# The last 96 rows of a weight matrix: one load of ScalarE, or six loads of GpSimd with unequal shares

## The chip, the cores and the metric

The kernel runs on one core of a Trainium2 chip. The metric is the device time of one launch in microseconds (us). The engines are called as in the profile: PE is TensorE's matmuls, PEld its weight loads, DVE is VectorE, ACT is ScalarE, POOL is GpSimd, SP is SyncE. Sixteen DMA engines move data between the chip's memory and the core's on-chip memory. The text calls them "DMA engines" throughout, to keep them apart from the compute engines that issue the loads.

## The reference

A decode step for two tokens (B = 2, D = 512) adds three terms: the input, an attention over a cache, and a bilinear feed-forward block.

```
xn = layernorm(x)
q  = xn @ wq                                  # 32 heads of 128
k, v = the last 2048 positions of the caches  # per token and head
A  = softmax(q k^T / sqrt(128)) v @ wo        # wo: 4096 x 512
g, u = xn @ w_gate, xn @ w_up                 # 512 x 1376
out = x + A + (g * u) @ w_down                # w_down: 1376 x 512
```

Everything is float32. w_down has 1376 = 10 * 128 + 96 rows: ten blocks of 128 rows, and a rest of 96. The change is about how those 96 rows get onto the chip.

## The kernel before

Nearly all inputs are laid out by the host into one array `stream`, in the order in which the kernel wants them. `loads()` lists the pieces: each entry is a load number, a tile (`step0` to `step2`, or `extra`) and its fields (two or three heads of the caches, slices of wq, wo, w_down). `issue()` puts these loads on SP's queue. A load is [128, up to 13824] float32, one long row for each of 128 partitions, spread over all 16 DMA engines. A load into a `step` tile has to wait on SP until that tile's last use has ended, so three loads at most are open at a time.

The compute engines follow the stream. For each head DVE multiplies the keys by q (`products`) and sums (`sums`), every fourth head gives the softmax weights of a group (`weights`, with ACT's exponentials), and PE multiplies the weights by the values (`weigh`) and adds the output projections into one accumulator `acc` in PSUM (`wo`, `down`). The stream ends with load 24, which is cut into five pieces so that little work is left behind the last one: the value rows of the last head, four blocks of wo, and blocks 1 to 9 of w_down. After the last piece there are a few small matmuls, a copy and the store of the result.

Three small things are not in `stream`. `x_nat`, the two rows of x, goes to the tile `xr`. `wd_rest`, the last 96 rows of w_down, goes to the tile `wr` (96 partitions, 2 KB in each). Both are loaded from ACT's queue, ahead of ACT's first computation. `wr` has one reader: the matmul in `turn()`, `add_rows(hT[:FR, ...], wr, 0)`, which adds those rows' share to `acc` in the third step of the loop, once the feed-forward block's hidden values `hT` are there.

`Program` records every operation and finds its dependences from the tiles' regions; `emit()` writes them out per engine, in the order recorded, with a semaphore for every load. A reader of a tile that several loads fill waits for each of those loads. All instructions are issued by two lines of `emit()`, so the profile gives them one line number, L198 (L199 in the changed kernel, which is one line longer above it).

Of the kernel before, what the change touches and what calls it, by code (L numbers as in the profile page):

```python
# [10 lines left out]
P = 128  # L11
B, D, H, DH, SK, F = 2, 512, 32, 128, 8192, 1376
# [7 lines left out]
NFC = F // P  # L20
# [7 lines left out]
M = 4 * N  # L28
CK, CO = J * DH, D
CX = B * NC + 4 * N + 4 * HG + 2 * NFB + 2 + B  # L30
BUFS = 3
WIDTH = 13824
WIDTH_X = 4096
# [2 lines left out]
def loads():  # L36
# [6 lines left out]
    def wq(g, *cs):  # L43
        return units("wq", *[(g, c) for c in cs])
# [8 lines left out]
    for n in range(6, 20):  # L53
# [29 lines left out]
    out = [  # L83
        (0, "x", [("c", 0, CX)] + wq(0, 0, 1, 2, 3)),
        (1, 0, big[1] + small[1]),
# [150 lines left out]
def build(nc, stream, x_nat, wd_rest, out):  # L236
    pr = Program(nc)
    pe, dve, act, pool = pr.pe, pr.dve, pr.act, pr.pool

    buf = [pr.sb(f"step{i}", [P, WIDTH]) for i in range(BUFS)]  # L240
    buf_x = pr.sb("extra", [P, WIDTH_X])
    xr = pr.sb("xr", [P, D])
    wr = pr.sb("wr", [FR, D])
# [7 lines left out]
    xnb = pr.sb("xnb", [P, NC, P])  # L251
    cst = pr.sb("cst", [P, CX])
    p_all = pr.sb("p", [P, 2, HG, JG, M])
# [22 lines left out]
    for n, t, fields in loads():  # L276
# [8 lines left out]
        src = stream[pos : pos + P * (c1 - c0)].rearrange("(p i) -> p i", p=P)  # L285
# [3 lines left out]
    def issue(upto):  # L289
        while queue and queue[0][0] <= upto:  # L290
            _, dst, src = queue.pop(0)
            pr.load("SP", dst, src)

    issue(3)
    pr.load("ACT", wr, wd_rest)
    dve.memset(mean_w, 1.0 / D)
    dve.memset(eps_t, EPS)
    dve.memset(ones, 1.0)
# [2 lines left out]
    for t in (xr, zero, mt, both, p_all):  # L301
        pool.memset(t, 0.0)
    pr.load("ACT", xr[:B, :], x_nat)

    c0 = got["c", 0]
    dve.tensor_copy(cst, c0)
# [264 lines left out]
    a, b, c, d = GROUPS[g]  # L571
# [31 lines left out]
def laid_out(x):  # L603

    import numpy as np

    a = x["A_x"].reshape(B, D)
    xs = np.zeros((P, CX), a.dtype)
    xs[:, : B * NC] = a.reshape(B, P, NC).transpose(1, 0, 2).reshape(P, B * NC)
    o = B * NC  # L610
    for r in range(4):
        for n in range(N):
            xs[4 * n + r :: 32, o + r * N + n] = 1.0
    o += 4 * N
    for n in range(HG):
        for q in range(4):
            xs[32 * q + n, o + 4 * n + q] = 1.0
    o += 4 * HG
    for n in range(NFB):
        for b in range(B):  # L620
            xs[32 * n + b, o + n * B + b] = 1.0
    o += 2 * NFB
    for j in range(4):
        for b in range(B):
            xs[32 * j + b, o + b] = 1.0
    xs[:, o + 2 :] = a[:, 0]
    cache = {
        kind: x[name][:, :, SK - W :, :].reshape(B, H, HB, J * DH).transpose(1, 0, 2, 3)
        for kind, name in (("k", "A_k_cache"), ("v", "A_v_cache"))
    }  # L630
    wq = x["A_wq"].reshape(P, NC, H * DH)
    wo = x["A_wo"].reshape(H, P, D)
    gu = {
        kind: x[name].reshape(P, NC * F)
        for kind, name in (("wg", "B_w_gate"), ("wu", "B_w_up"))
    }
    wd = x["B_w_down"]

    def field(kind, i):
        if kind == "c":  # L640
            return xs
        if kind in ("k", "v"):
            return cache[kind][i].reshape(P, CK)
        if kind == "wq":
            g, c = i
            return wq[:, c, g * HG * DH : (g + 1) * HG * DH]
        if kind == "wo":
            return wo[i]
        if kind == "wd":
            return wd[i * P : (i + 1) * P]  # L650
        return gu[kind]

    parts = [
        np.concatenate([field(kind, i) for kind, i, _ in fields], axis=1).ravel()
        for _, _, fields in loads()
    ]
    return {"stream": np.concatenate(parts), "x": a, "wd_rest": wd[NFC * P :]}


_INS = ["A_x", "A_k_cache", "A_v_cache", "A_wq", "A_wo", "B_w_gate", "B_w_up", "B_w_down"]  # L660
# [24 lines left out]
```

## Time and profile before

| what | value |
|---|---|
| median of 3 runs | 377.32 us (377.32 to 377.57) |
| the profiled execution | 377.64 us |
| its span, first to last instruction | 376.3 us |
| outside the span (377.64 - 376.3) | 1.3 us |
| busy: DVE, PE, ACT, POOL | 80%, 50%, 4%, 1% of the span |
| moved by the DMA engines | 159.66 MB, mean 424 GB/s |

The profile is one execution's page, with views that answer questions about parts of it. The views used below are the page's list of DMA queues, which gives packets, megabytes and the share of 16 DMA engines' time for each queue (also for a part of the span alone); the timeline, which lists instructions in order; the windows, which give each engine's busy time, the DMA engines' busy share and the rate for stretches of the span; and the chain of work that ended last. In the timeline a bracket at the end of a row tells how long the engine had been idle and what ended that. Queue q1 is SP's, q10 is ACT's; q8 and q14 bring instructions, not data.

### The profile page before, as it was taken

What the parts mean: (1) busy time and instruction counts of PE and PEld (TensorE: products, weight loads), DVE (VectorE), ACT (ScalarE), POOL (GpSimd) and SP (SyncE); (2) the same over time, 40 slices, a digit from 0 to 9 for tenths busy, and PEclk for the clock granted to TensorE, in tenths of its full rate; (3) what the DMA queues carried; (4) which work ended last, traced back from release to release, by engine and by line L of the source; (5) the groups of instructions that cost most, each with busy time, mean ns of one, the idle gap of its engine ahead of it and who ended that gap; (6) DMA issues with size and microseconds to landing.
All of it is one profiled execution on the core that took longest, in us unless ns stands there. A gap on an engine that the chain in (4) does not pass through costs nothing.

```text
span 376.3 us, 1954 instructions
## 1 busy us (share of the span) xinstructions
PE 189.3 (50%) x844; PEld 56.8 (15%) x844; DVE 302.8 (80%) x165; ACT 14.5 (4%) x28; POOL 2.6 (1%) x9
## 2 busy tenths in 40 slices
PE   0651747703762355617446383462657335243976
PEld 0210122100220011102121020110111012000312
DVE  3059979999999988899599499969969997999401
ACT  1000100000000000000000000000000001000100
POOL 2000000000000000000000000000000000000000
PEclk9956966876665658768555856858566685565999
DMA  8999899998999989999999999999999999999995
GB/s 324 470 394 488 376 470 411 431 470 377 464 435 417 464 382 460 453 400 464 394 448 453 406 458 400 447 454 406 453 420 419 445 447 434 441 402 411 432 416 235
DMA packets 4443, 159.66 MB, mean 424 GB/s; under 512 B 498, under 2 KB 626, under 8 KB 980
## 3 DMA queue, kind: packets, MB, share of 16 engines
q1 hardware_dynamic: 4320, 159.35, 98.5%
q10 hardware_dynamic: 116, 0.20, 0.1%
q8 instruction: 6, 0.10, 0.1%
q14 instruction: 1, 0.01, 0.0%
HBM read 159.49 MB, written 0.07 MB: 424 GB/s over the span
## 4 chain that ended last, share of the span: by engine, by line
DMA 49%; DVE 42%; PE 6%; issue 2%; another core or an unknown queue 1%; SPq 0%; DVEq 0%
DMA step<-in_stream_dram 49%; DVE step L198 22%; DVE s L198 19%; PE q L198 3%; PE o_ps L198 2%; PE acc L198 2%; PE tr L198 0%; DVE both L198 0%; DVE nm L198 0%; DVE h_sb L198 0%; DVE rec L198 0%; SPq L198 0%; DVE mt L198 0%; DVE o_out L198 0%
## 5 line engine op out<-in xcount | busy, mean ns | idle before, releaser
L198 DVE TENSOR_TENSOR step<-step,q 128x4096 f32<-128x4096 f32 x32 | 141.1, 4408 | 37.3 <-DMA step<-in_stream_dram 37.3
L198 DVE TENSOR_REDUCE s<-step 128x32 f32<-128x4096 f32 x32 | 141.4, 4418 | 0.8
L198 PE MATMUL o_ps<-step,p 128*32 128x512 f32 x496 | 94.8, 869 | 69.8 <-DMA step<-in_stream_dram 68.2
L198 PE MATMUL q<-step,xnb 128*128 128x512 f32 x56 | 41.4, 877 | 26.9 <-DVE step L198 19.7
L198 PE MATMUL acc<-step,oT 128*2 128x512 f32 x64 | 23.6, 926 | 42.2 <-DVE oT L198 28.5
L198 PEld LDWEIGHTS o_ps<-step,p 128*32 128x32 f32 x496 | 20.4, 147 | 126.8 <-DMA step<-in_stream_dram 74.9
L198 PEld LDWEIGHTS q<-step,xnb 128*128 128x128 f32 x56 | 13.4, 267 | 54.5 <-DVE step L198 24.9
L198 ACT ACTIVATE p<-s,zero 64x128 f32<-64x128 f32 x16 | 6.4, 399 | 268.1 <-DVE s L198 268.0
L198 DVE TENSOR_TENSOR oT<-gu,rec 128x8 f32<-128x8 f32 x8 | 1.3, 158 | 14.8 <-PE gu L198 14.8
L198 PE MATMUL tr<-both,ones 128*128 128x24 f32 (+1 forms) x18 | 4.8, 348 | 15.7 <-DVE both L198 15.7
L198 PE MATMUL gu<-step,xn 128*2 128x512 f32 (+1 forms) x48 | 8.5, 647 | 7.5 <-DMA step<-in_stream_dram 7.5
L198 PE MATMUL gu<-cst,o_sb 128*128 128x8 f32 x64 | 10.1, 285 | 3.1 <-ACT o_sb L198 3.1
L198 PEld LDWEIGHTS gu<-cst,o_sb 128*128 128x128 f32 x64 | 9.4, 225 | 10.6 <-ACT o_sb L198 8.9
L198 PEld LDWEIGHTS acc<-step,oT 128*2 128x2 f32 x64 | 1.5, 82 | 53.0 <-DVE oT L198 29.1
L198 PEld LDWEIGHTS tr<-both,ones 128*128 128x128 f32 x18 | 3.8, 262 | 26.6 <-DVE both L198 26.6
L198 PE MATMUL q<-extra,xnb 128*128 128x512 f32 x8 | 6.2, 947 | 1.9 <-DVE xnb L198 1.9
L198 DVE TENSOR_REDUCE nm<-tr 64x4 f32<-64x8 f32 x16 | 2.6, 163 | 5.4 <-PE tr L198 5.3
L198 ACT COPY o_sb<-o_ps 128x512 f32<-128x512 f32 x8 | 4.7, 585 | 46.0 <-PE o_ps L198 46.0
L198 PE MATMUL gu<-cst,h_sb 128*128 128x6 f32 x8 | 1.9, 362 | 5.6 <-DVE h_sb L198 5.6
L198 PE MATMUL tr<-st,mean_w 128*128 128x4 f32 x2 | 0.6, 365 | 7.5 <-DVE st L198 7.5
L198 PEld LDWEIGHTS gu<-step,xn 128*2 128x2 f32 x48 | 2.0, 93 | 14.7 <-DMA step<-in_stream_dram 9.1
L198 DVE TENSOR_REDUCE both<-p 128x8 f32<-128x256 f32 x8 | 3.3, 413 | 0.6 <-ACT p L198 0.6
(52 smaller groups left out, 39.8 us busy)
## 6 DMA issues: line engine op xcount, KB each, us to landing
step<-in_stream_dram SPq DMA_DIRECT2D x17, 6912.0 KB, 31.2
step<-in_stream_dram SPq DMA_DIRECT2D x2, 6400.0 KB, 29.5
step<-in_stream_dram SPq DMA_DIRECT2D x1, 6656.0 KB, 35.9
step<-in_stream_dram SPq DMA_DIRECT2D x1, 5504.0 KB, 34.4
step<-in_stream_dram SPq DMA_DIRECT2D x1, 4608.0 KB, 23.8
extra<-in_stream_dram SPq DMA_DIRECT2D x1, 2048.0 KB, 28.3
step<-in_stream_dram SPq DMA_DIRECT2D x1, 2048.0 KB, 24.8
step<-in_stream_dram SPq DMA_DIRECT2D x2, 1024.0 KB, 19.6
```

The costliest lines, as they stand in the source:

```text
L198: ins = getattr(e, method)(*args, **kw)
```

## The change

The one load of `wr` from ACT's queue is taken out. In its place POOL issues six loads, behind its five memsets. They fill 30, 8, 2, 22, 4 and 30 partitions of `wr`. The source of each is written as `(j i) d -> i j d`, which cuts its rows over 3, 2, 2, 2, 4 and 3 DMA engines, 16 in all, and the host reorders the rows of `wd_rest` to match. If each load goes on from the DMA engine at which the one before it ended, every DMA engine carries one share: three get 10 rows each, then two 4, two 1, two 11, four 1, three 10. Before, the 96 rows were cut evenly, 6 for each.

```diff
+REST = ((3, 30), (2, 8), (2, 2), (2, 22), (4, 4), (3, 30))
...
     issue(3)
-    pr.load("ACT", wr, wd_rest)
     dve.memset(mean_w, 1.0 / D)
...
     for t in (xr, zero, mt, both, p_all):
         pool.memset(t, 0.0)
     pr.load("ACT", xr[:B, :], x_nat)
+    lo = 0
+    for k, m in REST:
+        src = wd_rest[lo : lo + m, :].rearrange("(j i) d -> i j d", i=k)
+        pr.load("POOL", wr[lo : lo + m, :], src)
+        lo += m
...
-    return {"stream": np.concatenate(parts), "x": a, "wd_rest": wd[NFC * P :]}
+    rest, lo = [], NFC * P
+    for k, m in REST:
+        rest.append(wd[lo : lo + m].reshape(k, m // k, D).transpose(1, 0, 2).reshape(m, D))
+        lo += m
+    return {"stream": np.concatenate(parts), "x": a, "wd_rest": np.concatenate(rest)}
```

POOL's whole work in the kernel's body, before:

```order
L198 MEMSET xr 128x512
L198 MEMSET zero 128x1
L198 MEMSET mt 128x32
L198 MEMSET both 128x24
L198 MEMSET p 128x2048
```

and the end of it in the changed kernel:

```order
L199 MEMSET both 128x24
L199 MEMSET p 128x2048
L199 DMA wr<-in_wd_rest_dram 30x1x512
L199 DMA wr<-in_wd_rest_dram 8x1x512
L199 DMA wr<-in_wd_rest_dram 2x512
L199 DMA wr<-in_wd_rest_dram 22x1x512
L199 DMA wr<-in_wd_rest_dram 4x512
L199 DMA wr<-in_wd_rest_dram 30x1x512
```

The six loads stand behind everything else that POOL does; nothing is queued behind them.

PE around the one reader of `wr`, with what each row waits for (`s_d` with a number is the semaphore of one load), before:

```order
L198 MATMUL gu<-cst,h_sb 128x6 [waits s_DVE]
L198 MATMUL gu<-cst,h_sb 128x6 x3
L198 MATMUL q<-step,xnb 128x512 [waits s_d3]
L198 MATMUL acc<-wr,hT 2x512 [waits s_d4,s_DVE]
L198 MATMUL q<-step,xnb 128x512 x2
```

and in the changed kernel:

```order
L199 MATMUL gu<-cst,h_sb 128x6 [waits s_DVE]
L199 MATMUL gu<-cst,h_sb 128x6 x3
L199 MATMUL q<-step,xnb 128x512 [waits s_d3]
L199 MATMUL acc<-wr,hT 2x512 [waits s_d19,s_d18,s_d20,s_d17,s_d21,s_d16,s_DVE]
L199 MATMUL q<-step,xnb 128x512 x2
```

PE's order is the same; the matmul that reads `wr` waits for six loads where it waited for one. On ACT the load of `wr` is gone and the load of `xr` is the first instruction; DVE's and SP's orders are unchanged.

## The prediction

> **What bounds the kernel now.** I read the page's list of DMA queues first, then the windows over the whole span. The first shows how the 16 DMA engines' time is used (packets, MB, share of their time), the second whether they are ever idle (the last two columns are the DMA engines' busy share and GB/s; a transfer is counted where it starts).
>
> ```profile
> q1 hardware_dynamic: 4320, 159.35, 98.5%
> q10 hardware_dynamic: 116, 0.20, 0.1%
> ...
> 52.00:371.00 319.00, 164.36 (x721) 47.25 (x724) 271.07 (x139) 11.07 (x24) 0.00 (x0) 0.68 1.00 430
> ```
>
> SP's stream holds the DMA engines 98.5% of the time, and from 52 to 371 us their share is 1.00: no gap. So the time is the stream's bytes at the DMA engines' rate, a start and a tail. Compute matters only if it keeps SP from issuing. It doesn't, by the lead of the loads (KB each, us from issue to landing):
>
> ```profile
> step<-in_stream_dram SPq DMA_DIRECT2D x17, 6912.0 KB, 31.2
> ```
>
> 6912 KB are 7.08 MB, 16.5 us at 430 GB/s; landing after 31.2 us means that a load lies queued for some 14.7 us behind the one in flight. Compute can be late by about that before the DMA engines see it.
>
> The end is in the timeline, the result's last four instructions:
>
> ```profile
> 372.69 0.84 PE L198 MATMUL q<-step,hT 128*2 128x128 f32 x24
> 373.72 0.33 PEld L198 LDWEIGHTS q<-step,hT 128*2 128x2 f32 x16 [0.48 <-DMA step<-in_stream_dram]
> 373.72 0.62 PE L198 MATMUL q<-step,hT 128*2 128x128 f32 x16 [0.19 <-DMA step<-in_stream_dram]
> 374.41 0.29 DVE L198 COPY o_out<-q 128x128 f32<-128x128 f32 x1 [1.99 <-PE q L198]
> 374.73 0.35 SPq L198 DMA_DIRECT2D out_dram<-o_out  x1
> ```
>
> The last matmuls wait for the last piece of the stream, which lands just before 373.72; what follows is fixed. A load has landed when the slowest of its DMA engines is done, so the question is whether all 16 are done together. The windows at the end say no:
>
> ```profile
> 371.00:371.60 0.60, 0.60 (x8) 0.00 (x0) 0.00 (x0) 0.00 (x0) 0.00 (x0) 1.00 0.93 376
> 371.70:372.25 0.55, 0.00 (x0) 0.00 (x0) 0.52 (x1) 0.00 (x0) 0.00 (x0) 1.00 0.45 183
> 372.25:372.75 0.50, 0.27 (x12) 0.27 (x16) 0.17 (x1) 0.00 (x0) 0.00 (x0) 1.00 0.42 172
> 372.75:373.68 0.93, 0.78 (x31) 0.47 (x20) 0.00 (x0) 0.00 (x0) 0.00 (x0) 1.00 0.09 35
> ```
>
> From about 371.7 the share is 0.45 to 0.42 of 16, about seven DMA engines; nine have nothing left. The seven go on until the share falls to 0.09, so they end about 1 us after the nine. Which work made seven late? The list of queues for 6.3 to 371 us:
>
> ```profile
> q1 hardware_dynamic: 3889, 156.86, 99.7%
> q8 instruction: 6, 0.10, 0.1%
> q14 instruction: 1, 0.01, 0.0%
> ```
>
> Seven packets that are not the stream's: six instruction fetches of 16 KB and one of 8 KB. Seven fetches and seven late DMA engines: the simplest reading is one fetch each, six long delays and one shorter. The stream itself is even (128 rows on 16), and so were the 96 rows.
>
> **The change, part by part.** I add to the profiled execution, 377.64 us with a span of 376.3; it is 0.3 above the median of 377.32, so differences are carried over to the median.
>
> *a. The rows on the late DMA engines.* What one 2 KB row costs a DMA engine has two rows: the stream's (98.5% of 376.3 x 16 is 5930 us for 159.35 MB, 37 us per MB), and ACT's queue in the first 7 us, where the 96 rows and the two of x went:
>
> ```profile
> q10 hardware_dynamic: 116, 0.20, 8.1%
> ```
>
> 8.1% of 7.0 x 16 is 9.1 us for 0.20 MB, 45 us per MB. So a row costs 0.076 to 0.093 us. Six DMA engines get 1 row in place of 6, two get 4, eight get 10 or 11. If the six are the ones with the long fetches, and one of the two with 4 rows has the short fetch, the last to end saves 5 x 0.076 to 5 x 0.093, 0.38 to 0.46: I take **-0.42**. What is late next: the nine others get up to 5 rows more, 0.46, and had about 1 us of margin, so they don't take over. The pieces before the last one (values, wo, w_down) come off the same DMA engines and land earlier by as much, so the 0.19 us that PE had in hand at 373.72 is kept.
>
> *b. The first load without company.* SP's first load, 1057 KB of x, constants and wq, shared its DMA engines with the 96 rows:
>
> ```profile
> extra<-in_stream_dram SPq DMA_DIRECT2D x1, 1057.0 KB, 5.9
> ...
> 2.70:3.80 1.10, 0.00 (x0) 0.00 (x0) 0.12 (x1) 0.37 (x1) 0.44 (x1) 1.00 0.94 389
> 3.80:5.30 1.50, 0.00 (x0) 0.00 (x0) 0.00 (x0) 0.00 (x0) 0.00 (x0) 1.00 1.04 368
> ```
>
> It ran at 368 to 389 GB/s, not 430. If the small rows were the reason, its 1.08 MB take 2.5 us in place of 2.9: up to -0.42, for all DMA engines, since the rows then come between long rows. If its own shorter rows are the reason, nothing. The trace doesn't tell; I lean to the second and take **-0.1**.
>
> *c. Completions.* Six loads end where one did. If every DMA engine reports each of them, that is 5 more tiny packets on each. The nearest row is the very end, 372.5 to 376.3 us, where nearly all packets are small:
>
> ```profile
> q1 hardware_dynamic: 169, 0.14, 10.9%
> ```
>
> 10.9% of 3.8 x 16 is 6.6 us, 0.039 us a packet, of mostly 512 bytes and more. Five cost 0 to 0.2; I take **+0.1**.
>
> [...]
>
> *d. Issue and waits.* The load that goes (us to landing, then the issue on ACT), POOL's last memset, and the reader of `wr` on PE:
>
> ```profile
> wr<-in_wd_rest_dram ACTq DMA_DIRECT2D x1, 192.0 KB, 5.5
> ...
> 0.73 0.41 ACTq L198 DMA_DIRECT2D wr<-in_wd_rest_dram  x1
> ...
> 1.34 1.80 POOL L198 MEMSET p<- 128x2048 f32 x1
> ...
> 56.91 1.86 PE L198 MATMUL acc<-wr,hT 96*2 96x512 f32 x2 [2.47 <-DVE hT L198]
> ```
>
> POOL is free from 3.14 us and the rows are wanted at 56.91, when `hT` comes: 53 us. The load took 5.5 us to land from ACT's queue; six in a row from POOL, even at that time each, are there by 36 us. Were a row to be served only between two rows of the stream (55 KB at 37 us per MB, 2.06 us), 11 rows take 23 us more than that, about 59: then PE would wait some 2 us, with q's matmuls and the next softmax behind it, still inside the 14.7 us of lead. [...] ACT loses one issue of 0.41 us ahead of a wait; the first load's arrival a little earlier meets DVE, which then waits for the second load anyway:
>
> ```profile
> 6.64 0.20 DVE L198 COPY cst<-extra 128x66 f32<-128x66 f32 x1 [3.83 <-DMA extra<-in_stream_dram]
> ...
> 23.05 4.42 DVE L198 TENSOR_TENSOR step<-step,q 128x4096 f32<-128x4096 f32 x1 [13.11 <-DMA step<-in_stream_dram]
> ```
>
> All zero. **Sum:** -0.42 - 0.1 + 0.1 = -0.42, 377.64 to 377.22; from the median, **376.9 us**. About 0.2%, 0.75 us, is what a measurement of this kernel can tell from no change, so this counts as the same.
>
> **The rivals.**
>
> *Slower: each visit costs.* A queue that a DMA engine serves rarely may cost it more than its bytes. The fetches are the only such visits here; from 140 to 160 us there is one:
>
> ```profile
> q1 hardware_dynamic: 172, 8.63, 100.0%
> q8 instruction: 1, 0.02, 0.3%
> ```
>
> 0.3% of 20 x 16 is 0.96 us (0.8 to 1.1 by rounding), for 16 KB that the stream's rate moves in 0.61: 0.2 to 0.5 more. If each of the six loads, with its share or its completion, costs each DMA engine that, the stream ends 1.2 to 3.0 later, less the 0.42 saved: 378.1 to 379.9. It decides from 0.2 us a visit ((0.75 + 0.42) / 6). For it: POOL's queue is unused in the trace, and how its loads are served is unknown. Against: ACT's rows, also from a second queue, cost 0.093 each and no more. [...]
>
> *The same, the wrong way: the shares fall elsewhere.* No view numbers the DMA engines. If a late one gets 10 or 11 rows, it ends 4 or 5 rows later, 0.30 to 0.46, and with the completions 377.7 to 377.9. For it: nothing in the trace places the shares, and the fetches may not fall alike in each execution. Against: the fetches' count, six long, meets six shares of one row, and two of four leave room for the short one. That the loads are not cut as written (evenly after all) belongs here too: 377.3 to 377.5. [...]
>
> *Faster.* If (b) is whole, the row costs 0.093 and completions little: -0.46 - 0.42 + 0.05 = -0.83, 376.5.
>
> **How the numbers follow.** Forecast 0.43, shares elsewhere 0.16, costly visits 0.24, faster 0.17. Only the rival on (b) passes 0.2% below: faster 0.17. Only costly visits pass it above: slower 0.24. Same: 0.43 + 0.16 = 0.59. The range goes from 376.4, which takes in nearly all of the faster case, to 378.4, the lower part of costly visits; what is left out is the rest of that case and a little below, about 0.18.
>
> **What would show it.** In the profile after: queue q10 shrinks to x's two rows, and POOL's queue appears with 0.20 MB. Right on (a): in the last windows before the result the share no longer sits at 0.45 for 1 us; the drop from 0.9 is steeper and the last matmuls start near 373.3. Right on (b) or not: DVE's first copy, 6.64 before, and the rate around 3 to 5 us. Right on (d): the matmul on `wr` still starts at 56.9, or later with no gap in the DMA share afterwards. Costly visits would show as a DMA share below 1 or a lower rate in the first 60 us, and all later landings shifted by the same 1 to 3 us. Shares elsewhere: the same or a longer half-idle stretch at the end. A second stretch of idle DMA engines in mid-span would make the whole account wrong.

## The result, and the profile after

The changed kernel takes 379.21 us (median of 6 runs, 379.01 to 379.52) where the kernel before takes 377.45 (6 runs beside it, 377.32 to 377.70). The ratio is 1.0048, with a 95% interval of 1.0035 to 1.0061: slower by 1.8 us. The forecast was 376.9 with a range of 376.4 to 378.4, so it missed on both counts. The profiled execution took 379.21 us with a span of 377.9, 1.6 more than before.

The page's list of DMA queues (packets, MB, share of the 16 DMA engines' time):

```profile
span 377.9 us, 1961 instructions
...
q1 hardware_dynamic: 4320, 159.35, 98.4%
q0 software_dynamic: 416, 0.20, 0.2%
q8 instruction: 6, 0.10, 0.1%
q14 instruction: 1, 0.01, 0.0%
q10 hardware_dynamic: 4, 0.00, 0.0%
```

The rows moved from ACT's queue q10 to POOL's, q0, as said. By their own packets they still cost next to nothing, 0.2% of the DMA engines' time. SP's stream is the same bytes in the same number of packets, and it takes the same share of a span that is 1.6 us longer: the stream itself became slower. The windows tell where. The first row is the kernel before, the others the changed kernel; the last two columns are the DMA engines' busy share and GB/s:

```profile
6.30:58.00 51.70, 25.80 (x76) 9.08 (x76) 34.60 (x21) 2.16 (x3) 0.00 (x0) 0.75 1.00 434
```

```profile
6.30:58.00 51.70, 24.98 (x74) 8.91 (x74) 32.00 (x17) 2.16 (x3) 0.37 (x1) 0.72 1.01 421
52.00:372.00 320.00, 158.99 (x721) 45.56 (x721) 271.06 (x139) 11.08 (x24) 0.00 (x0) 0.69 1.00 431
```

In both kernels the DMA engines are busy without a gap from 6.3 to 58 us, but they move 421 GB/s in place of 434; (434 - 421) / 434 of 51.7 us is 1.5 us. From 52 us on the rate is 431, as before (430). So the loss lies where POOL's rows move, and it is no idle time. The windows count a transfer where it starts, and one 55 KB row of all 16 DMA engines is 17 GB/s in this stretch, so the size of the loss is taken from the packets further down. The timeline of the changed kernel shows the same from the compute engines' side:

```profile
3.10 3.57 POOL L199 DMA_DIRECT2D wr<-in_wd_rest_dram  x6
...
5.81 0.20 DVE L199 COPY cst<-extra 128x66 f32<-128x66 f32 x1 [2.99 <-DMA extra<-in_stream_dram]
...
54.51 4.42 DVE L199 TENSOR_TENSOR step<-step,q 128x4096 f32<-128x4096 f32 x1 [3.47 <-DMA step<-in_stream_dram]
...
59.08 1.86 PE L199 MATMUL acc<-wr,hT 96*2 96x512 f32 x2 [2.48 <-DVE hT L199]
...
375.32 0.62 PE L199 MATMUL q<-step,hT 128*2 128x128 f32 x16 [0.17 <-DMA step<-in_stream_dram]
...
376.32 0.35 SPq L199 DMA_DIRECT2D out_dram<-o_out  x1
```

The first load of the stream arrives 0.83 us earlier (6.64 before). The multiplication on load 3's keys starts at 54.51; before, its row was this:

```profile
52.34 4.42 DVE L198 TENSOR_TENSOR step<-step,q 128x4096 f32<-128x4096 f32 x1 [2.25 <-DMA step<-in_stream_dram]
```

That is 2.2 us later, after a start 0.8 earlier. The reader of `wr` still waits for `hT`, not for the rows; it shifts with load 3's arrival. The last matmuls start 1.60 us later, and the store with them.

The end is less even than before:

```profile
371.70:372.70 1.00, 1.00 (x16) 0.11 (x8) 0.00 (x0) 0.00 (x0) 0.00 (x0) 1.00 0.95 387
372.70:373.70 1.00, 0.58 (x8) 0.00 (x0) 0.35 (x1) 0.00 (x0) 0.00 (x0) 1.00 0.65 264
373.70:374.30 0.60, 0.20 (x8) 0.20 (x12) 0.34 (x1) 0.00 (x0) 0.00 (x0) 1.00 0.34 137
374.30:375.27 0.97, 0.85 (x32) 0.54 (x22) 0.00 (x0) 0.00 (x0) 0.00 (x0) 1.00 0.07 30
```

The share goes from 0.95 over 0.65 and 0.34 to 0.07. The first DMA engines have nothing left 2.4 us before the last is done; before it was 1.9.

**One DMA engine at a time.** No view numbers the DMA engines, but the trace has a record for each packet (queue, size, start, duration), and on one DMA engine a packet starts where the one before it ends (as a rule 3 ns before that end). Chaining them so gives 16 chains; now and then two of them are confused. I use two numbers of each: when its first long row of the stream (55 KB) starts, and how long it takes from there to the start of its 28th long row, 57.5 to 58.0 us into the kernel before (eight of the 27 rows between are of 44 KB). In us:

```
kernel           first 55 KB row    from there to the 28th, by DMA engine
before           5.67 to 6.12       51.83 to 51.86, all 16
after            4.93 to 5.47       53.54 to 53.71  those with no row of wr (five; a sixth is unclear)
                                    53.97  with 4 rows      54.13  with 5 rows
                                    54.35 to 54.54  with 10 to 12 rows
```

Two things stand here. A DMA engine that carries rows is later by about 0.075 us a row, the predicted size ((54.45 - 53.62) / 11). And **every** DMA engine, also one that carries nothing, needs about 1.75 us more than before. That second term was not in the sum. The experiments ask what it is. The first theories were a price for each packet of POOL's queue (1.75 / 26 is 0.067 us), for each load (1.75 / 6 is 0.29) or for each packet of a DMA engine that has nothing to send, against a price of the rows themselves when they meet the long ones. The theory that held came only with e6.

### The profile page after: what moved, and what is told of

The parts are those of the page before. It is cut to its first block, busy times and chain, and to the rows that moved or that the text cites. A ratio compares the mean times of both kernels' runs of the same rounds, so it can differ in the third digit from the quotient of the medians.

```text
span 377.9 us, 1961 instructions
## 1 busy us (share of the span) xinstructions
PE 183.9 (49%) x844; PEld 54.2 (14%) x844; DVE 302.7 (80%) x165; ACT 14.5 (4%) x28; POOL 6.1 (2%) x15
## 4 chain that ended last, share of the span: by engine, by line
DVE 55%; DMA 40%; PE 2%; issue 1%; another core or an unknown queue 1%; SPq 0%; DVEq 0%
DMA step<-in_stream_dram 40%; DVE step L199 27%; DVE s L199 26%; DVE both L199 1%; PE acc L199 1%; PE tr L199 1%; DVE mt L199 0%; DVE nm L199 0%; DVE mtt L199 0%; DVE mc L199 0%; DVE h_sb L199 0%; PE q L199 0%; DVE rec L199 0%; DVE oT L199 0%
## 5 line engine op out<-in xcount | busy, mean ns | idle before, releaser
L199 PE MATMUL q<-step,xnb 128*128 128x512 f32 x56 | 38.8, 826 | 33.4 <-DVE step L199 22.2
L199 PE MATMUL acc<-step,oT 128*2 128x512 f32 x64 | 22.7, 883 | 43.8 <-DVE oT L199 29.5
L199 PE MATMUL gu<-step,xn 128*2 128x512 f32 (+1 forms) x48 | 9.8, 734 | 7.9 <-DMA step<-in_stream_dram 7.9
L199 PE MATMUL gu<-cst,o_sb 128*128 128x8 f32 x64 | 8.4, 258 | 3.1 <-ACT o_sb L199 3.1
L199 PEld LDWEIGHTS gu<-cst,o_sb 128*128 128x128 f32 x64 | 7.7, 191 | 10.8 <-ACT o_sb L199 8.9
L199 PE MATMUL q<-extra,xnb 128*128 128x512 f32 x8 | 5.2, 807 | 1.9 <-DVE xnb L199 1.9
```

The costliest lines, as they stand in the source:

```text
L199: ins = getattr(e, method)(*args, **kw)
```

## The experiments

All times are medians in us; the ratio is to the kernel before, run beside it (377.37 to 377.46), with its 95% interval.

| kernel | time | ratio |
|---|---|---|
| e1, one load by POOL | 377.96 | 1.0014 (1.0005 to 1.0023) |
| e2, six plain loads by POOL | 378.29 | 1.0024 (1.0015 to 1.0034) |
| e3, six plain loads by ACT | 378.24 | 1.0025 (1.0015 to 1.0035) |
| e4, one load by ACT, late | 377.74 | 1.0010 (1.0001 to 1.0018) |
| e5, one load in SP's stream | 377.58 | 1.0007 (0.9998 to 1.0015) |
| e6, before and 12 loads of one row | 377.50 | 1.0004 (0.9995 to 1.0013) |
| e7, before and 32 rows on two DMA engines | 378.04 | 1.0018 (1.0009 to 1.0026) |
| e8, after in four loads | 378.95 | 1.0044 (1.0030 to 1.0058) |
| e9, before and 12 tiny loads | 377.54 | 1.0001 (0.9992 to 1.0010) |
| e10, rows inside the first load | 377.32 | 0.9996 (0.9988 to 1.0005) |
| e11, e5 with 128 partitions | 377.40 | 0.9998 (0.9989 to 1.0007) |
| e12, e7's load by ACT | 378.04 | 1.0014 (1.0005 to 1.0023) |
| e13, 32 rows to their DMA engines' own partitions | 377.44 | 1.0001 (0.9992 to 1.0010) |
| e14, 32 rows to other DMA engines' partitions | 378.69 | 1.0034 (1.0022 to 1.0046) |

### The change, taken apart: e1 to e4

e1: one load of all 96 rows, by POOL.

```diff
-    pr.load("ACT", wr, wd_rest)
...
+    pr.load("POOL", wr, wd_rest)
```

> The 96 rows in one load of POOL, cut evenly (6 rows on each DMA engine). Visits theory (each packet of POOL's queue costs each DMA engine 0.067 us, 26 of them in the changed kernel, 1.75 us): about 4 packets a DMA engine, +0.3, rows 6 x 0.085 = +0.5, the first load without company -0.8: 377.4, no change. Per-load theory (1.75 / 6 = 0.29 a load): the same, 377.4. Rival, the use of POOL's queue as such costs the 1.75 us once: 378.9.

e2: six loads by POOL, with the changed kernel's rows each, but not cut by `(j i) d -> i j d`.

```diff
-    for k, m in REST:
-        src = wd_rest[lo : lo + m, :].rearrange("(j i) d -> i j d", i=k)
-        pr.load("POOL", wr[lo : lo + m, :], src)
+    for m in (30, 8, 2, 22, 4, 30):
+        pr.load("POOL", wr[lo : lo + m, :], wd_rest[lo : lo + m, :])
```

> The six loads of POOL without the cut over a few DMA engines: 30, 8, 2, 22, 4, 30 rows in their own order, at most 2 rows on a DMA engine per load. Visits theory: one packet of rows and one completion per load, 12 in place of 26: +0.8; some 7 or 8 rows on a late DMA engine +0.64; first load -0.8: 378.1. Per-load theory: six loads cost 1.75 as in the changed kernel: 379.0.

e3: the same six plain loads, by ACT, at the place of the old one.

```diff
-    pr.load("ACT", wr, wd_rest)
+    lo = 0
+    for m in (30, 8, 2, 22, 4, 30):
+        pr.load("ACT", wr[lo : lo + m, :], wd_rest[lo : lo + m, :])
+        lo += m
```

> The same six plain loads from ACT's queue in place of POOL's. If the cost is POOL's queue alone: as before but for one or two rows more on some late DMA engine, 377.5 to 377.7. Rival, six small loads cost the DMA engines whoever issues them (completions): 378.5 to 379.2.

e4: the old single load, still by ACT, but issued behind ACT's square root, so that it moves beside the long rows instead of beside the first load.

```diff
-    pr.load("ACT", wr, wd_rest)
...
+    pr.load("ACT", wr, wd_rest)
```

> One load of the 96 rows from ACT's queue as before, but issued behind ACT's square root (8.8 us), so that the rows come among the long rows of the stream. If only POOL's queue costs: the first load alone saves 0.8, the rows cost 0.5 later: 377.2. Rival, any packet of a second queue among long rows costs 0.067: 7 packets, +0.47: 377.6.

Measured: 377.96, 378.29, 378.24, 377.74. Six plain loads cost the same from ACT as from POOL, which speaks against POOL's queue as the cause; in e3, though, the first 30 rows still move beside the first load, so e7 and e12 below are the cleaner pair. e2 fell between its two forecasts (378.1 and 379.0), e3 between its own. One load costs something too when it meets the long rows, from either queue (377.96 and 377.74 against 377.37); an expectation of about 377.4 for e1 and 377.2 for e4 fell. Per DMA engine, the way to the 28th long row takes 52.90 to 53.05 in e1 and 52.56 to 52.78 in e4, 51.85 before: 6 rows each cost 0.8 to 1.1, not 6 x 0.08. The step from e2 to the change (378.29 to 379.21, not run together) is the rearranged cut, which puts 10 to 12 rows on some DMA engines and none on others.

### Where the rows stand, and how often a queue is visited: e5 to e8

e5: the rows as a load of SP's own stream, behind load 1. `issue(1)` issues loads 0 and 1, so the rows stand behind the stream's second load, not its first; in the trace they move at 21.0 to 22.6 us.

```diff
-    issue(3)
-    pr.load("ACT", wr, wd_rest)
+    issue(1)
+    pr.load("SP", wr, wd_rest)
+    issue(3)
```

> The 96 rows on SP's own queue, between the first and the second load of the stream. No second queue meets the first load or the long rows. If the first load ran slowly because of the 96 rows beside it: -0.25 (0.8 saved at its end, 0.5 spent behind it): 377.2. If its own shorter rows are the reason: 377.45, no change.

e6: the kernel before, and twelve more loads by POOL, of one row each, into a tile that a small DVE copy reads much later.

```diff
+    idle = pr.sb("idle", [FR, D])
+    idle_1 = pr.sb("idle_1", [FR, 1])
...
+    for i in range(12):
+        pr.load("POOL", idle[i : i + 1, :], wd_rest[i : i + 1, :])
...
+        dve.tensor_copy(idle_1[:12, :], idle[:12, 0:1])
```

> The kernel before with the load of ACT kept, and 12 more loads of POOL, one row of 2 KB each into a spare tile, which the builder cuts into 16 pieces of 128 bytes, one for each DMA engine (a small copy on DVE reads them before the 96 rows' matmul). Hardly any bytes: the cost of the queue alone. Visits theory: one piece and one completion per load, 24 packets a DMA engine, 24 x 0.067 = 1.6: 379.1. Per-load theory: 12 x 0.29 = 3.5: 381.0. POOL's queue costing once: 379.2, and no more for the twelve than for one.

e7: the kernel before, and one more load by POOL, of 32 rows cut over two DMA engines.

```diff
+    pr.load("POOL", idle[:32, :], wd_rest[:32, :].rearrange("(j i) d -> i j d", i=2))
...
+        dve.tensor_copy(idle_1[:32, :], idle[:32, 0:1])
```

> The kernel before with the load of ACT kept, and one more load of POOL: 32 rows of 2 KB cut over two DMA engines, 16 rows on each, into a spare tile. The other 14 carry no rows. Visits theory with fillers (every DMA engine takes as many packets as the one with most): 8 packets and a completion on each, 9 x 0.067 = 0.6: 378.05, and DMA engines without rows are late by 0.6 at 58 us. Per-load theory: 0.29, 377.75. No fillers: the 14 take one packet each, +0.07.

e8: the changed kernel with another cut in four loads.

```diff
-REST = ((3, 30), (2, 8), (2, 2), (2, 22), (4, 4), (3, 30))
+REST = ((3, 30), (7, 14), (6, 48), (4, 4))
```

> The changed kernel with four loads in place of six: 30 rows on 3 DMA engines, 14 on 7, 48 on 6, and 4 plain. The two DMA engines that carried 11 rows and an instruction fetch each now carry 2. Visits theory: 5 + 1 + 4 + 1 packets and 4 completions, 15 in place of 26: 1.0 us. The latest is then a DMA engine with a fetch and 8 rows: -0.8 + 1.0 + 0.7 = +0.9, 378.3. Per-load theory: 4 x 0.29 = 1.2: 378.5. If rows on the late DMA engines don't matter: 378.5 to 378.7.

Measured: 377.58, 377.50, 378.04, 378.95. e6 is the clearest: twelve loads more than before, each with a visit and a completion on every DMA engine, and nothing lost that can be told from none (1.0004, 0.9995 to 1.0013). Its queue by the page:

```profile
q0 software_dynamic: 384, 0.03, 0.1%
```

384 packets are 24 for each of 16 DMA engines, nearly as many as the change has (416, or 26). So neither the number of loads nor of packets is the price. One single load of 32 rows, e7, costs more than those twelve. Its 378.04 is what the theory of visits with fillers forecast (378.05); e12 below shows that this was by luck. And four loads cost as much as six (e8 and the change, 1.0044 and 1.0048, each inside the other's interval); e8's forecasts, 378.3 to 378.7, were all too low. What the dear runs share is rows, and few DMA engines that send them. e5 stays within what can be told from no change, but its 52.89 to the 28th long row shows the same loss as e1 and e4, about 1.04 for 6 rows each, most of it made good by first long rows that start 0.9 earlier (5.03 on average); the idea that rows in SP's own queue cost only their bytes, about 377.2, fell as well.

In e6 three of the 16 DMA engines took 52.34 to 52.38 to the 28th long row, the other 13 took 51.95 to 51.99. Its rows were cut in 16 pieces, one from every DMA engine, but they were written to partitions 0 to 11 only, 4 partitions for each of three DMA engines, if the long loads share partitions out by fours, which no record tells; those three lost 0.4 for 4 rows each. That pointed from who sends a row to where it lands.

### Fillers, shape, and the queue: e9 to e12

In the changed kernel q0 has 26 packets on each DMA engine, also on those without rows: the rows go two to a packet of 4096 bytes (44 packets, and 8 of a single row), and a DMA engine with less to send than the busiest has packets of 8 bytes in their place (228 of them; 40 of 4 bytes in place of a single row). The other 96 are completions of 4 bytes, 16 for each of the six loads. e9 asks what those cost: the kernel before and twelve loads by POOL, of 2 rows of 128 bytes.

```diff
+    for i in range(12):
+        pr.load("POOL", idle[:2, 40 * i : 40 * i + 32], wd_rest[2 * i : 2 * i + 2, :32])
...
+        dve.tensor_copy(idle_1[:2, :12], idle[:2, :480].rearrange("p (i w) -> p i w", w=40)[:, :, 0])
```

> The kernel before with the load of ACT kept, and 12 more loads of POOL of two rows of 128 bytes into a spare tile. Two DMA engines carry one piece of each, the other 14 one 8-byte filler and one completion of each: 24 packets without bytes. Fillers theory (0.06 us for each filler): +0.7, 378.1. Rows theory (the time goes with the 2 KB rows, not with the packets beside them): 377.4 to 377.5.

e10: the 96 rows, padded to 128, become 512 more columns of SP's first load, so there is no load of `wr` at all.

```diff
-        (0, "x", [("c", 0, CX)] + wq(0, 0, 1, 2, 3)),
+        (0, "x", [("c", 0, CX)] + wq(0, 0, 1, 2, 3) + units("wr", 0)),
...
-    wr = pr.sb("wr", [FR, D])
...
-    pr.load("ACT", wr, wd_rest)
...
-        add_rows(hT[:FR, NFC % 4, NFC // 4, :], wr, 0)
+        add_rows(hT[:FR, NFC % 4, NFC // 4, :], got["wr", 0][:FR], 0)
```

> The 96 rows, padded to 128, as 512 more columns of SP's first load: no rows of 2 KB, no second queue, each row of the first load 10.5 KB in place of 8.5. Rows theory: the first load's DMA engines are free at about 5.5 us in place of 5.85, and nothing is lost later: -0.35, 377.0 to 377.1. If the rows cost the same however they come: 377.4 to 377.6.

e11: e5, but with the rows padded to 128, so that the load has the partitions of the long loads.

```diff
-    wr = pr.sb("wr", [FR, D])
+    wr = pr.sb("wr", [P, D])
...
+    issue(1)
+    pr.load("SP", wr, wd_rest)
...
-        add_rows(hT[:FR, NFC % 4, NFC // 4, :], wr, 0)
+        add_rows(hT[:FR, NFC % 4, NFC // 4, :], wr[:FR], 0)
```

> As the run with the 96 rows on SP's queue behind the first load, but with the tile and the load padded to 128 partitions, 8 rows of 2 KB on each DMA engine, cut as all long loads are. Partitions theory (a row costs twice because it goes to a partition that another DMA engine serves in the long loads): no second cost now, 8 x 0.085 = 0.7 in place of 1.04, 377.2 to 377.3. If short rows as such cost 0.17 each: 8 x 0.17 = 1.4, 377.9 to 378.0.

e12: e7's load of 32 rows, issued by ACT behind its square root instead of by POOL.

```diff
+    pr.load("ACT", idle[:32, :], wd_rest[:32, :].rearrange("(j i) d -> i j d", i=2))
...
+        dve.tensor_copy(idle_1[:32, :], idle[:32, 0:1])
```

> The run with 32 more rows on two DMA engines, with ACT issuing that load (behind its square root) in place of POOL: no fillers, and no packet at all on the 14 other DMA engines. Fillers theory: the 14 keep their time, the two are 1.4 to 1.6 later, 377.4 to 377.6. Rows theory: all 14 are later by 0.5 as with POOL, 377.9 to 378.1.

Measured: 377.54, 377.32, 377.40, 378.04. The page's row for e9's extra loads:

```profile
q0 software_dynamic: 384, 0.00, 0.1%
```

Again 24 packets on every DMA engine, and a ratio of 1.0001. By the packets' records the fillers are here of 4 bytes, twelve on each of 14 DMA engines, beside twelve completions. To the 28th long row the DMA engines take 51.95 to 52.04, 0.1 to 0.2 more than before: 24 such packets together cost about 0.12 us, 0.005 each. e12 takes away e7's fillers, which are of 8 bytes, and keeps the rows (ACT's queue sends no fillers: its page has 150 packets on q10, the 116 of before, 32 rows and 2 completions), and it costs what e7 costs, 378.04 both times. Fillers are out. e10 is below the kernel before by no more than can be told from none, and above its forecast (377.0 to 377.1).

e11 against e5 changes the partitions, and carries more bytes, 8 rows on each DMA engine in place of 6. To the 28th long row it takes 52.37, half the loss of e5 (0.52 against 1.04); that is 0.065 a row, the price of the bytes. The long rows right behind the small ones show it best: in e5 the first 44 KB row of most DMA engines takes 2130 to 2200 ns, in e11 1627 on every one, and 1627 to 1635 in the kernel before. The times, 377.40 and 377.58, have overlapping intervals, so here it is the packets' records that tell the two apart, not the medians.

e12's chains fall in three groups: two take 53.87 (they carry 16 rows each), six take 52.55 to 52.73, eight take 52.34 to 52.44. The rows go to partitions 0 to 31, which by fours are eight DMA engines: the two that carry and the six. The six lose 0.2 to 0.3 more than the eight, for 4 rows that land on each. That is the grouping that e6 had suggested.

### Whose partitions: e13 and e14

These two differ in one number. Both are the kernel before, and four more loads by ACT, behind its square root, of 8 rows on two DMA engines each; 16 rows on each of two DMA engines in all, read much later by a small DVE copy. In e13 they go to partitions 0 to 7 and 32 to 39, in e14 to 64 to 71 and 96 to 103. That the two carriers fill the first of these in the long loads, and two other DMA engines the second, was an assumption that no run had shown by then.

```diff
+    idle = pr.sb("idle", [P, 2, D])
...
+    for i in range(4):
+        lo = 0 + 32 * (i % 2)        # e14: lo = 64 + 32 * (i % 2)
+        src = wd_rest[8 * i : 8 * i + 8, :].rearrange("(j i) d -> i j d", i=2)
+        pr.load("ACT", idle[lo : lo + 8, i // 2, :], src)
```

> [...] Partitions theory: the 14 other DMA engines keep their time (52.0 us from the first long row to 58 us, where the run into partitions 0 to 31 had 52.4 to 52.7), the two are 1.0 to 1.4 later; 377.4 to 377.6. If any short row slows all DMA engines: 378.0 as there.

> The same four loads from the same rows, into partitions 64 to 71 and 96 to 103, which two other DMA engines serve. Partitions theory: all 14 others are later by some 0.5, the two that serve those partitions by more; 378.0 to 378.3. If the partition doesn't matter: as the run before, whatever that is.

Measured: 377.44, ratio 1.0001 (0.9992 to 1.0010), against 378.69, 1.0034 (1.0022 to 1.0046), on the same chip. The same rows, number of loads, packets and queue, so the page's row is one and the same for both:

```profile
q10 hardware_dynamic: 156, 0.27, 0.2%
```

The timelines differ at the last matmuls. e13, then e14:

```profile
373.52 0.62 PE L198 MATMUL q<-step,hT 128*2 128x128 f32 x16 [0.17 <-DMA step<-in_stream_dram]
```

```profile
374.71 0.62 PE L198 MATMUL q<-step,hT 128*2 128x128 f32 x16 [0.20 <-DMA step<-in_stream_dram]
```

By DMA engine, to the 28th long row, in us:

```
kernel    two that carry 16 rows    two more          the other twelve
before    -                         -                 51.83 to 51.86 (all 16)
e13       53.22                     none apart        51.80 to 51.85 (fourteen)
e14       53.54, 53.55              53.12, 53.14      52.07 to 52.12
```

In e13 only the two carriers pay, 1.37 us for 16 rows, 0.086 a row: the price that the prediction took. Nobody else notices. In e14 two DMA engines that carry none of these rows lose 1.28 us, nearly as much as if they had carried 16 rows, and the other twelve lose 0.23, half of the 0.5 that was expected. The two carriers lose 0.33 more than in e13. The fetches that the chains place fall on other DMA engines than the carriers in both runs. The late end of e14 is that of one of the two hit ones, on which the chains put a fetch too (its long rows end at 356.4, no other's past 355.6). That meeting is chance, and without it e14 would have ended some 0.8 us earlier (an estimate, 356.4 less 355.6); it is why e14 lies above its forecast, and why the price is read from the chains and not from the two medians.

So in e14 a row sent by one DMA engine into partitions that another one fills in the long loads delays that other one by about its own time, and all by a little. No record tells which DMA engine fills a partition in the long loads; I read it from who is hit: three in e6 (12 partitions), eight with the carriers in e12 (32), nobody but the two carriers in e13 (0 to 7 and 32 to 39), two others in e14 (64 to 71 and 96 to 103). Four neighbouring partitions for each DMA engine, and four more 32 further on, would fit all four runs; that is an estimate from them.

Two limits belong to this. No run let the DMA engines of partitions 64 to 71 write there themselves; that partitions from 64 on are dear whoever writes them is made unlikely only by e6 and e12, whose rows land below 32. And the price for each landed row does not add up where rows land nearly everywhere: in e1 and e5 the rows go to partitions 0 to 95, which is eight rows for each of eight DMA engines and four for each of the others, if that sharing out holds for all of them. At 0.08 a row that would be 0.32 us apart, but e1's chains lie within 0.15 of each other, and most of e5's within 0.06. There nearly the whole extra loss is even.

## Why the prediction was wrong, point by point

- **What bounds the kernel** was right. The DMA engines' share stays at 1.00, the end waits for the last piece of the stream, and no new wait came: the reader of `wr` still waits for `hT`, 2.48 us where it was 2.47.
- **(a), the rows on the late DMA engines, is the step that failed**, by a term that it left out. Its price, 0.076 to 0.093 a row, holds for the DMA engine that carries a row (0.075 after, 0.086 in e13). The sum took this as the whole cost. But it is only what the sender's own packets show. The six loads let ten DMA engines write into partitions 0 to 95, by the sharing out estimated above some of everybody's, beside long rows, and each of the 16 lost about 1.75 us, in the long rows' own durations: the 55 KB packets are longer on all DMA engines, by some 200 ns each at 12 to 16 us, beside the first load's rows, and by 80 to 130 at 44 to 52 us, beside the last load's, and as before once the small rows are through. At 24 to 26 us, where only the two rows of a plain load move, the 44 KB packets take 1632 ns, against 1629 before. That it depends on where the rows land is shown by e11 against e5 and e14 against e13; how it comes to 1.75 on every DMA engine is not.
- **The trace of the kernel before held a sign of it.** The prediction's argument that ACT's rows cost 0.093 each and no more looked at the rows' own packets alone, as (a) did. In the kernel before the rows move ahead of all 55 KB packets, but the price stands in the first load's packets of 8456 bytes: 320 ns each from 2.8 to 3.7 us, the first of the time in which the rows move (2.7 to 5.4), and 377 to 392 on average from 4.0 to 5.5. In the changed kernel, where no row of `wr` moves then, they average 321 to 339 from 3.0 to 5.0.
- **The aim of (a) failed as well.** The six lightest shares were to meet the six long fetches. That rival, shares elsewhere, came true beside the other. The loads cut by the rearrangement go on from where the last one stopped, but the plain ones of 2 and of 4 rows start again at the first DMA engine (their rows sit on the chains that also carry x's two rows). The shares are 10 to 12 rows on eight DMA engines, 5 and 4 on two, and none on six. Of the five long fetches that the chains place, one fell on a DMA engine without rows, one on one with 4, and three on 10 or 11. That seven late DMA engines are those with a fetch was read rightly: in the kernel before their chains end 372.7 to 373.3, the other nine at 371.4 to 371.8. The price was read too small, 0.96 us from the queue's row and about 1 us from the windows: a fetch costs its DMA engine 1.55 us (16 KB) or 0.97 (8 KB). In the changed kernel the three with 10 or 11 rows and a fetch end their long rows last (356.8 to 356.9; 355.3 with 10 rows and no fetch, 356.1 with a fetch and no rows).
- **(b), the first load without company**, had the right sign and the wrong lean. The first long row starts 0.77 us earlier (5.91 to 5.14 on average). Six rows at 0.076 to 0.093 are 0.46 to 0.56 of that, which leaves 0.21 to 0.31 for (b) in place of 0.1. Its own shorter rows were not the reason: without rows beside them they take 320 ns for 8456 bytes, 38 us per MB, as the long ones do (37).
- **(c), completions**, 0.1, came out about right by luck: e9's 24 small packets on every DMA engine, completions among them, cost 0.12. That is 0.005 each in place of 0.039, but the changed kernel has more of them than the five that were counted: six completions on each DMA engine where there was one, and the fillers.
- **(d), issue and waits**, zero, was right. The matmul on `wr` starts 0.05 to 0.06 us after `hT`'s copy has ended, with one load to wait for (56.86 to 56.91) and with six (59.02 to 59.08).
- **The sum again**, for the DMA engine that ends last: its first long row starts 1.1 earlier, all lose 1.75, its own 11 rows cost 0.94. That is +1.6, and the last matmuls start 1.60 later. The forecast took a gain of 0.52 from the first and the third together, with 1 row in place of 11, and had nothing for the second, which turns the sign.
- **The rival of costly visits** had the sign, the size (1.2 to 3.0 less 0.42) and the marks in the profile: a lower rate in the first 60 us, all later landings shifted. That was luck, for its mechanism fell: visits, completions, fillers and POOL's queue cost nothing that the times show (1.0004 in e6, 1.0001 in e9, 378.04 in e12 as in e7). Twelve more loads of POOL cost under 0.5 us in all (e6 and e9, upper ends of the intervals 1.0013 and 1.0010).

What stays open: why DMA engines that neither carry such a row nor have it land in their partitions are slowed too. It is 0.23 us in e14, about 0.5 in e12, and in the changed kernel the larger part of 1.75. It is not peculiar to the rearranged cut, for in e2 the one DMA engine without rows takes 52.84 to its 28th long row, 0.99 more than before. In the changed kernel the 96 rows land on partitions 0 to 95, by the same estimate 8 rows or 4 for each DMA engine, at 0.08 a row 0.3 to 0.6, an estimate. What the unequal shares alone would bring, without rows in other DMA engines' partitions, was not run.

## What to carry to other kernels

When one long stream keeps the DMA engines busy, give a small load the stream's own shape: 128 partitions (e11, which lost 0.52 us to the 28th long row where e5 with 96 partitions lost 1.04), or a few more columns of a load that is there already (e10, 377.32, ratio 0.9996 with 0.9988 to 1.0005: no measurable gain over the kernel before, but no loss, and one load less). Loads of other shapes cost more here than their own packets show, because they delay other DMA engines (in e14 two by 1.28 us and twelve by 0.23, none of which carried a row); look at how long the stream's own packets take while the small ones move, not at the small queue's share. And a plan that hands shares to single DMA engines needs proof of where they land, since here the loads of 2 and of 4 rows did not go on where the last one ended, but started again at the first.

## What the runs showed of the hardware

- In e14 32 rows of 2 KB, sent by two DMA engines into partitions 64 to 71 and 96 to 103 beside the stream, delayed two others by 1.28 us each (0.08 a row, if 16 landed on each) and the other twelve by 0.23 each. In e13, into partitions 0 to 7 and 32 to 39, they cost the two senders alone, 1.37 us each. Where 96 rows land on partitions 0 to 95 the extra loss is nearly even: e1's 16 DMA engines lie within 0.15 us of each other, most of e5's within 0.06.
- POOL's loads that gave some DMA engines nothing sent them packets of 4 or 8 bytes, as many as the busiest had (with the completions 26 packets on each of 16 in the changed kernel); twelve of 4 bytes with twelve completions cost 0.12 us (e9).
- In the kernel before a 16 KB instruction fetch took 1.55 us from its DMA engine, an 8 KB one 0.97. Seven of them left the end of an otherwise even stream uneven by 1.9 us, first to last.
